# Weight conversions in twos with low parts on VectorE, gates in three steps, fillers out of S and Y, and a new planned order

## The chip, the cores and the metric

The kernel runs on one core of a Trainium2 chip, as one launch. The metric is the device time in microseconds (us). Three runs of the kernel before took 453.63, 475.21 and 476.38 us; their median is 475.21. The chip's engines work side by side, each through its own queue in order: TensorE (PE in the profile: matmuls; PEld is its weight load), VectorE (DVE), ScalarE (ACT), GpSimd (POOL), and SyncE (SP), whose queue issues the DMA transfers.

## The reference

Three computations follow each other. All inputs are float64 or float32 arrays that are computed to better than one float32 product; hence the high and low parts below.

```
# 1. mLSTM, batch 2, 8 heads, 768 steps, head width 40
m_new = max(f + m, i);  f' = exp(f + m - m_new);  i' = exp(i - m_new)
C = f' * C + i' * v k^T;   n = f' * n + i' * k
y = sigmoid(o) * (C q) / max(|n . q|, 1)
# 2. x = y as [1536, 320];  w1, w2: [320, 1024], w3: [1024, 1024], w_out: [1024, 320]
x = ((x @ w1) * (x @ w2)) @ w3 @ w_out
# 3. w_in: [320, 2048], w_out2: [2048, 320]
h = x @ w_in;   out = (h * tanh(softplus(h))) @ w_out2
```

## The kernel before, in words

**Attention in chunks.** The recurrence is cut into 6 chunks of 128 steps for each of the 2 batches: 12 units, u = 0 to 11, each with all 8 heads. The gates (running maximum, decay, sums) are scanned by VectorE once, chunk 0 first and then the other 640 columns (`part`, L612). For each unit TensorE runs these steps, in program names:

- E (L399 to L405): four matmuls of 512 columns write the exponents of the decay matrix, `psE`. Their right side `ex_r` is written per chunk by `rb` (L636). ScalarE exponentiates (`dw`).
- S (L420): eight products of keys and queries, `psS`; VectorE multiplies with the decay (`wg`).
- I (L435): what the state gives, `psI`. U (L448): the state's update, `psU`, from `vw`, which GpSimd computes; VectorE adds it to the state `st`.
- Y (L471): eight products with the values, `psY`, 41 columns each. VectorE adds I's part, ScalarE and VectorE make the divisor, GpSimd multiplies with gate and divisor (`xo`, L498: two multiplications, then a cast and a subtraction on 64 columns).
- X (L506): three transpositions, `psX`; ScalarE and VectorE split the result into a high part `hs` and a low part `ls`.

**Products.** Each fp32 product is computed as a sum of products of fp32r high and low parts. A and B (L763, L771) are x times w1 and x times w2, 8 matmuls of 512 columns each (`mm320`, L749), for 3 blocks of 4 units and 8 column groups: 24 of either. W (L722) multiplies w3 by w_out beforehand (`psw`). X1 (L785) multiplies the product of A and B with that (`psx`). H (L844, `psh`) and O (L860, `pso`) are the third computation, 48 of each, with the Mish function on ScalarE between them and one subtraction on VectorE (`gl`).

**Conversions.** Weights come as float64 words. A piece of up to 384 columns (`add_piece`, L272) is loaded by DMA (`raw`, 4 buffers), its magnitude taken (`mag`, ScalarE or VectorE) into a buffer `f` (5 buffers), clamped, put together bit by bit in three more VectorE steps (`bits1`, `bits2`, `bits3`, L296 to L309), rounded to its high part by ScalarE (`high`, L311), and subtracted by GpSimd to give the low part (`low`, L315), which frees `f`. There are 80 pieces: 16 of w1 and w2, 8 of w_out, 24 of w3, 16 of w_in2, 16 of w_out2.

**Order.** A planner (`Work`, L41) holds a node per step, with an engine, a due time (from the table `TUNE`), an assumed duration, the nodes it needs and the buffers it takes. It goes through assumed time and always picks the node that can start first, among near ones the one with the earliest due time; the order so found is emitted to each engine's queue. Where it foresees a gap on TensorE before the last X, it emits fillers (`keep_warm`, L370: matmuls of 512 columns into `psz` that nobody reads, L139 to L144). In units 0 to 5, two fillers stand inside each S and two inside each Y (L423, L474). Three more fillers stand at the start (`w0n`), after the constants that they read are made by GpSimd and ScalarE.

```
            for p in range(HP):
                if p % 2 and warm:
                    keep_warm(1)
```

## Time and profile before

| | |
|---|---|
| runs | 453.63, 475.21, 476.38 us (median 475.21) |
| profiled execution | span 474.30 us from the first to the last instruction, 0.91 less than the median; its own time is not listed |
| busy: PE, PEld | 457.97, 395.01 us |
| busy: DVE, ACT, POOL | 316.97, 196.18, 129.24 us |
| granted clock of TensorE, mean | 0.910 |

Times in the rows are from the span's start. A row of a timeline has the start, the length, the engine, the line of the kernel, the operation with the tile written and those read, the shape and the count of instructions in it; in square brackets stands idle time of the engine ahead of it, and what ended it. Matmuls overlap, so the time from one row's start to the next row's start tells what a step costs, rather than its length. A row of a window has its bounds and length, then for each engine the busy time and, in brackets, the number of instructions; then the mean granted clock of TensorE (1.00 is 2.4 GHz, 0.50 is 1.2 GHz), the share of the DMA engines and GB/s. A row of a group has the count, the busy time and the mean of one instruction in ns, and the idle time of the engine ahead of them.

### The profile page before, as it was taken

How to read it: one execution, taken by the hardware profiler on the slowest of the kernel's cores; microseconds unless marked ns; L12 is line 12 of the kernel's file. 1: busy time of each engine (PE TensorE's matmuls, PEld its weight loads, DVE VectorE, ACT ScalarE, POOL GpSimd, SP SyncE). 2: the span in 40 equal slices, each digit the busy share in tenths (PEclk: the TensorE clock that was granted, in tenths of full speed). 3: DMA queues.
4: the chain of work that ended last, by engine and by line, in shares of the span. 5: the costliest groups of instructions: out<-in, count | busy, mean ns of one | idle time of the engine just before them, and what ended most of it. 6: DMA issues, size and time to landing. Idle time of an engine off the chain costs nothing.

```text
span 474.3 us, 6843 instructions
## 1 busy us (share of the span) xinstructions
PE 458.0 (97%) x2498; PEld 395.0 (83%) x2498; DVE 317.0 (67%) x631; ACT 196.2 (41%) x404; POOL 129.2 (27%) x153
## 2 busy tenths in 40 slices
PE   7999899999889899999999999989999999999997
PEld 4687678888778789898888887869999999999996
DVE  5955856559997956887898999988994121131121
ACT  7465246533326363224443423854243322322320
POOL 3305634425645422232231252263230000000000
PEclk9659755569959999999999999999999999999999
DMA  7934435433340433233231343332301000010001
GB/s 221 273 96 122 124 117 152 123 94 119 112 117 29 141 115 100 90 102 109 78 107 62 100 134 101 101 112 75 107 29 56 2 0 1 0 57 0 1 0 55
DMA packets 31825, 41.90 MB, mean 88 GB/s; under 512 B 2160, under 2 KB 25968, under 8 KB 31792
## 3 DMA queue, kind: packets, MB, share of 16 engines
q1 hardware_dynamic: 31792, 41.48, 28.8%
q8 instruction: 19, 0.31, 0.3%
q14 instruction: 14, 0.11, 0.1%
HBM read 39.50 MB, written 1.97 MB: 87 GB/s over the span
## 4 chain that ended last, share of the span: by engine, by line
PE 45%; issue 4%; POOL 2%; DVE 1%; ACT 0%; POOLq 0%; ACTq 0%
PE pso L869 18%; PE psh L754 15%; POOL wil L212 2%; PE psa L754 2%; PE psb L754 2%; PE psx L794 2%; PE psx L796 2%; PE psx L795 2%; PE psw L729 1%; PE psx L798 1%; PE psx L799 1%; DVE pl L212 0%; DVE f L298 0%; DVE f L294 0%; DVE f L308 0%
## 5 line engine op out<-in xcount | busy, mean ns | idle before, releaser
L212 DVE TENSOR_TENSOR gl<-u,gh 128x512 fp32r<-128x512 f32 x48 | 33.9, 705 | 78.9 <-ACT u L854 76.3
L850 ACT ACTIVATE gh<-psh 128x512 fp32r<-128x512 f32 x48 | 28.6, 599 | 89.0 <-PE psh L754 85.2
L754 PE MATMUL psh<-hs,wih 128*128 128x512 f32 x144 | 56.1, 390 | 0.0
L303 DVE SCALAR_TENSOR_TENSOR f<-raw,f 128x384 int32<-128x384 int32 (+2 forms) x80 | 49.8, 623 | 1.6
L754 PE MATMUL psh<-hs,wil 128*128 128x512 f32 x144 | 48.4, 390 | 1.9 <-POOL wil L212 1.9
L308 DVE SCALAR_TENSOR_TENSOR f<-raw,f 128x384 int32<-128x384 int32 (+2 forms) x80 | 47.2, 591 | 1.3
L294 DVE TENSOR_SCALAR f<-f 128x384 f32<-128x384 f32 (+2 forms) x80 | 39.6, 500 | 7.7 <-ACT f L288 7.2
L869 PE MATMUL pso<-wo,gh 128*128 128x320 f32 x192 | 42.6, 310 | 0.0
L476 PEld LDWEIGHTS psY<-kv,w 128*128 128x128 f32 x192 | 36.9, 273 | 2.2 <-issue 0.2
L212 POOL TENSOR_TENSOR th<-f,th 128x384 fp32r<-128x384 f32 (+1 forms) x24 | 22.6, 940 | 57.8 <-ACT th L313 42.4
L298 DVE TENSOR_SCALAR f<-f 128x384 int32<-128x384 int32 (+2 forms) x80 | 36.7, 461 | 1.3
L754 PE MATMUL psh<-ls,wih 128*128 128x512 f32 x96 | 37.4, 389 | 0.0
L476 PE MATMUL psY<-kv,w 128*128 128x41 f32 x192 | 35.5, 350 | 0.0
L869 PEld LDWEIGHTS pso<-wo,gh 128*128 128x128 f32 x192 | 32.8, 188 | 1.4
L754 PEld LDWEIGHTS psh<-hs,wil 128*128 128x128 f32 x144 | 27.0, 188 | 7.9 <-POOL wil L212 2.3
L212 POOL TENSOR_TENSOR wil<-f,wih 128x384 fp32r<-128x384 f32 x16 | 23.5, 1473 | 34.5 <-ACT wih L313 31.8
L754 PE MATMUL psa<-hs,w12h 128*128 128x512 f32 x72 | 30.3, 421 | 2.0 <-DVE w L212 2.0
L729 PE MATMUL psw<-woh,th 128*128 128x320 f32 x128 | 29.2, 312 | 1.8 <-POOL th L212 0.8
L754 PEld LDWEIGHTS psh<-hs,wih 128*128 128x128 f32 x144 | 27.0, 188 | 4.3
L754 PE MATMUL psb<-hs,w12h 128*128 128x512 f32 x72 | 29.2, 405 | 1.4 <-ACT w L409 1.4
L869 PE MATMUL pso<-wo2h,gh 128*128 128x320 f32 x96 | 29.8, 310 | 0.0
L869 PE MATMUL pso<-wo2l,gh 128*128 128x320 f32 x96 | 29.7, 309 | 0.0
(131 smaller groups left out, 1054.7 us busy)
## 6 DMA issues: line engine op xcount, KB each, us to landing
raw<-in_w_dram SPq DMA_DIRECT2D x32, 384.0 KB
raw<-in_w_out_dram SPq DMA_DIRECT2D x24, 320.0 KB
raw<-in_w_in_dram SPq DMA_DIRECT2D x16, 384.0 KB
kv<-in_kv_dram SPq DMA_DIRECT2D x12, 324.0 KB
qk<-in_qk_dram SPq DMA_DIRECT2D x24, 160.0 KB
raw<-in_w_dram SPq DMA_DIRECT2D x8, 256.0 KB
sg<-in_o_gate_dram SPq DMA_DIRECT2D x12, 160.0 KB
out_dram<-yo SPq DMA_DIRECT2D x12, 160.0 KB
```

The source lines that it names most:

```text
L212: return eng.tensor_tensor(out=o, in0=a, in1=b, op=op)
L294: nc.vector.tensor_scalar(out=ff, in0=ff, scalar1=HI_MIN, scalar2=HI_MAX, op0=ALU.max, op1=ALU.min)
L298: nc.vector.tensor_scalar(out=f, in0=f, scalar1=3, scalar2=0x3FFFFFFF, op0=ALU.logical_shift_left, op1=ALU.bitwise_and)
L303: nc.vector.scalar_tensor_tensor(out=f, in0=t["raw"][:, :, 1], scalar=-0x40000000, in1=f, op0=ALU.bitwise_and, op1=ALU.bitwise_or)
L308: nc.vector.scalar_tensor_tensor(out=f, in0=t["raw"][:, :, 0], scalar=29, in1=f, op0=ALU.logical_shift_right, op1=ALU.bitwise_or)
L476: nc.tensor.matmul(ps[:, h * VW:(h + 1) * VW], lhsT=t["w"][:, h, :], rhs=t["v"][:, h, :], start=True, stop=True)
L729: nc.tensor.matmul(ps, lhsT=t[a][:, c * 128:(c + 1) * 128], rhs=wo[b], start=(c0 + c + s == 0), stop=(c0 + c == KC - 1 and s == 2))
L754: nc.tensor.matmul(ps, lhsT=a, rhs=b, start=(n == 0), stop=(n == len(seq) - 1))
L794: nc.tensor.matmul(x1ps[e], lhsT=wh, rhs=ph, start=first, stop=False)
L795: nc.tensor.matmul(x1ps[e], lhsT=wh, rhs=pl, start=False, stop=False)
L850: nc.scalar.activation(out=t["gh"], in_=t["ps"], func=AF.Mish)
L869: nc.tensor.matmul(ps, lhsT=t[a][:, sl], rhs=wo[b], start=(ft == 0 and n == 0), stop=(ft == KF2 - 1 and n == 2))
```

## The change

- Conversions go in twos: a piece is 768 columns (w1 with w2 of one column group, two groups of w_in2), 640 (two row groups of w_out or w_out2) or 512 (w3, in two parts per row group where there were three). 44 pieces instead of 80. There are 3 `raw` and 2 `f` buffers, each twice as wide; low and high parts of a piece lie in one tile.
- A table `ENG` names the engine of a step by kind of weight: low parts on VectorE but for those of w3, magnitudes on ScalarE but for w_out and the second half of w_out2.
- Gates come in three steps (chunk 0, chunk 1, chunks 2 to 5), with the subtraction that GpSimd did now on VectorE; `rb` is written in halves; the gates' i part of chunk 0 is loaded from ScalarE's queue.
- The cast and the subtraction of `xo` on GpSimd go; ScalarE copies the 64 columns (`dup`), X transposes them, and VectorE makes their low part behind X. The first multiplication (`xs`) no longer waits for the divisor.
- S and Y hold no fillers. Ten fillers at the start read a tile of zeros that VectorE writes; fillers in foreseen gaps fill 0.872 of the gap.
- The planner's assumed durations, its model of the clock and a common port for VectorE and GpSimd are changed, and all of `TUNE`: the order is new everywhere.

```diff
--- before.py
+++ after.py
...
-NRAW = 4
-NF = 5
+NRAW = 3
+NF = 2
...
-NW12A = 8
-NTH = 5
+NTH = 4
 
 TUNE = dict(
-    s_pe=0.286, s_act=0.0, s_dve=0.0, s_pool=0.0, warm=6, ahead=2, w0n=3, a0=134.03, ap=1.26,
...
+    s_pe=0.177, s_act=0.105, s_dve=0.071, s_pool=0.0, ahead=1, w0n=10, ff=0.872, ph=2.305, a0=134.03, ap=1.252,
+    a_ld=-435.054, e_e=599.147, e_s=206.636, e_r=43.484, rb=2, g_ld=-203.34, g1=-91.783, g2=-94.21, o_1=-391.129,
...
+
+ENG = dict(
+    mag_w12='ACT', mag_wo='DVE', mag_w3='ACT', mag_wi='ACT', mag_o2='ACT', mag_o3='DVE', lo_w12='DVE', lo_wo='DVE',
+    lo_w3='POOL', lo_wi='DVE', lo_o2='DVE', lo_o3='DVE', xo='POOL', vw='POOL', dup='ACT',
 )
...
+                    if self.port[n]:
+                        s = max(s, port)
...
-                while t + 2 * fill[1] < s:
-                    t, k = self.products(t, fill[1], 1.0), k + 1
+                stop = t + (s - t) * TUNE["ff"]
+                while t + 2 * fill[1] < stop:
+                    t, k = self.products(t, fill[1], 0.94), k + 1
...
-    def add_piece(due, lead, width, loads, outs, takes=(), gates=(), abs_act=True):
+    def add_piece(due, lead, width, loads, outs, takes=(), gates=(), kind=""):
...
+        mag_e, lo_e = ENG["mag_" + kind], ENG["lo_" + kind]
 
         def load():
-            t["raw"] = slot(cv, "raw", [128, 384, 2], I32)[:, 0:width]
+            t["raw"] = slot(cv, "raw", [128, 768, 2], I32)[:, 0:width]
             for o, i in loads(t["raw"]):
...
-            t["f"] = slot(cv, "f", [128, 384], I32)[:, 0:width]
-            if abs_act:
+            t["f"] = slot(cv, "f", [128, 768], I32)[:, 0:width]
+            if mag_e == "ACT":
                 nc.scalar.activation(out=t["f"].bitcast(F32), in_=t["raw"][:, :, 1].bitcast(F32), func=AF.Abs)
             else:
                 nc.vector.tensor_single_scalar(out=t["f"], in_=t["raw"][:, :, 1], scalar=0x7FFFFFFF, op=ALU.bitwise_and)
...
         def high():
-            t["h"], t["l"] = outs[0](), outs[1]()
-            nc.scalar.copy(t["h"], t["f"].bitcast(F32))
+            t["h"], t["l"] = outs()
+            nc.scalar.copy(t["h"], t["f"].bitcast(F32).rearrange("a (k c) -> a k c", k=t["h"].shape[1]))
 
         def low():
-            tt(nc.gpsimd, t["l"], t["f"].bitcast(F32), t["h"].bitcast(F32), sub)
...
-        add_node(("mag", n), "ACT" if abs_act else "DVE", due - 4, (0.41 if abs_act else 0.35) * e, mag,
-                 [("load", n), ("mag", n - 1)], [(places("f", NF), [("lo", n)])])
...
-        add_node(("lo", n), "POOL", due - 1, 0.96 * e, low, [("hi", n)])
+            eng = nc.gpsimd if lo_e == "POOL" else nc.vector
+            tt(eng, t["l"], t["f"].bitcast(F32).rearrange("a (k c) -> a k c", k=t["h"].shape[1]), t["h"].bitcast(F32), sub)
...
+        add_node(("lo", n), lo_e, due - 1, pool(width) if lo_e == "POOL" else dve(width), low, [("hi", n)], port=True)
         return n
...
-    def outs_of(pool, tag, name, width):
-        return [lambda p=p: pool().tile([128, width], F32R, tag=f"{tag}{p}", name=f"{name}{p}", bufs=1) for p in "hl"]
-
-    def cols(n, p):
-        return pieces[n][p].rearrange("a (c f) -> a c f", c=3)
+    def pair_outs(pool, tag, name, width):
+        def outs():
+            return [pool().tile([128, 2, width], F32R, tag=f"{tag}{p}", name=f"{name}{p}", bufs=1) for p in "hl"]
+        return outs
+
...
+
+        a, b = (identr, causal) if a is None else (a, b)
         ps = psum.tile([128, 512], F32, tag="b0", name="psz", bufs=1)
         for _ in range(n):
-            nc.tensor.matmul(ps, lhsT=identr, rhs=causal, start=True, stop=True)
+            nc.tensor.matmul(ps, lhsT=a, rhs=b, start=True, stop=True)
 
...
 
         def S_():
             t["S"] = [bank("psS") for _ in range(2)]
             for p in range(HP):
-                if p % 2 and warm:
-                    keep_warm(1)
                 for g in range(2):
                     rows = slice(64 * g, 64 * g + D)
...
         def Y():
             ps = t["Y"] = bank("psY")
             for h in range(H):
-                if h % 4 == 2 and warm:
-                    keep_warm(1)
                 nc.tensor.matmul(ps[:, h * VW:(h + 1) * VW], lhsT=t["w"][:, h, :], rhs=t["v"][:, h, :],
                                  start=True, stop=True)
...
-        def xo():
+        def xs():
             x = t["x"] = slot(att, "x", [128, 3 * T])
             xh = x[:, 0:DM].rearrange("a (h d) -> a h d", h=H)
-            tt(nc.gpsimd, xh, t["y"][:, :, 0:D], sg[kb, b][:, j % 2], mult)
-            tt(nc.gpsimd, xh, xh, t["r"].unsqueeze(2).to_broadcast([128, H, D]), mult)
-            nc.gpsimd.tensor_copy(out=x[:, DM:3 * T].bitcast(F32R), in_=x[:, R0:DM])
-            tt(nc.gpsimd, x[:, R0:DM], x[:, R0:DM], x[:, DM:3 * T], sub)
+            tt(nc.gpsimd if ENG["xo"] == "POOL" else nc.vector, xh, t["y"][:, :, 0:D], sg[kb, b][:, j % 2], mult)
+
+        def xo():
+            xh = t["x"][:, 0:DM].rearrange("a (h d) -> a h d", h=H)
+            tt(nc.gpsimd if ENG["xo"] == "POOL" else nc.vector, xh, xh, t["r"].unsqueeze(2).to_broadcast([128, H, D]), mult)
+
+        def dup():
+            x = t["x"]
+            if ENG["dup"] == "ACT":
+                nc.scalar.copy(x[:, DM:3 * T], x[:, R0:DM])
+            else:
+                (nc.vector if ENG["dup"] == "DVE" else nc.gpsimd).tensor_copy(out=x[:, DM:3 * T], in_=x[:, R0:DM])
...
+            half = slice(0, 64)
+            tt(nc.vector, h[half, 2, sl], p3[half, 2], h[half, 2, sl].bitcast(F32), sub)
...
+
+    STAGES = [(0, 1), (1, 2), (2, NCH)]
...
         def ld_g(c0, c1):
-            for dst, src in ((f, f_gate), (i, i_gate)):
-                nc.sync.dma_start(out=dst[:, c0 * T:c1 * T], in_=src[:, c0 * T:c1 * T])
+            for eng, dst, src in ((nc.sync, f, f_gate), (nc.sync if c0 else nc.scalar, i, i_gate)):
+                eng.dma_start(out=dst[:, c0 * T:c1 * T], in_=src[:, c0 * T:c1 * T])
 
         ld_g(0, 1)
+        nc.vector.memset(zr.bitcast(F32), 0.0)
...
+        nc.gpsimd.memset(qk[0][:, 0], 0.0)
...
-        nc.scalar.copy(identr, ident)
+        keep_warm(K["w0n"], zr[:, 0:128], zr)
...
         nc.scalar.copy(causal, z)
-        keep_warm(K["w0n"])
...
-        def rb(c):
+        def rb(c, e):
             sl = slice(c * T, (c + 1) * T)
+            hs = slice(4 * e, 4 * e + 4)
             if c >= K["rb"]:
...
-            tt(nc.vector, ex_r[c % 2][64:128], L2[64:128, sl].bitcast(F32).unsqueeze(1).to_broadcast([64, H, T]),
-               sel_h[64:128].unsqueeze(2).to_broadcast([64, H, T]), mult)
+            tt(nc.vector, ex_r[c % 2][64:128, hs], L2[64:128, sl].bitcast(F32).unsqueeze(1).to_broadcast([64, 4, T]),
+               sel_h[64:128, hs].unsqueeze(2).to_broadcast([64, 4, T]), mult)
...
+                add_node(("part", n), "DVE", due, 3 * dve(w) + dve(2 * w) + dve2(w) + (c[1] - c[0]) * dve(T), lambda c=c: part(*c),
+                         [("ld_g",), ("lb", n - 1)], port=True)
...
-    CH3 = [(0, 3), (3, 3), (6, 2)]
+    CH3 = [(0, 4), (4, 4)]
...
-        for i in range(KF2):
-            ft, x = divmod(i, 2)
-            wi_n[i] = add_piece(dues[i] - K["c_wi"], K["c_ld"], 384, cols_loads(w_in2, i),
-                                outs_of(w12_pool(ft), f"w{ft}_{x}", "wi", 384), gates=[("AB"[x], 2 * KF1 + ft)], abs_act=False)
...
+        for i in range(KF1):
+            n = add_piece(dues[2 * i] - K["c_wi"], K["c_ld"], 768, cols_loads([(w_in2, 2 * i), (w_in2, 2 * i + 1)]),
+                          pair_outs(w12_pool(i), f"w{i}", "wi", 384), gates=[(x, 2 * KF1 + i) for x in "AB"], kind="wi")
+            wi_n[2 * i], wi_n[2 * i + 1] = (n, 0), (n, 1)
...
```

How the order moves is seen at three places. The first is TensorE's queue at S of unit 0 and what follows (`psS`, `psU`, `psY` are the outputs of S, U and Y; `psz` those of fillers; `psg` transposes gates). Before:

```order
L427 MATMUL psS<-qk_78 128x128 x2
L374 MATMUL psz<-causal,identr 128x512
L427 MATMUL psS<-qk_78 128x128 x4
L374 MATMUL psz<-causal,identr 128x512
L427 MATMUL psS<-qk_78 128x128 x2
```

After:

```order
L463 MATMUL psS<-qk_78 128x128 x8
L414 MATMUL psz<-causal,identr 128x512 x4
L488 MATMUL psU<-vw,kv 40x41 x8
L414 MATMUL psz<-causal,identr 128x512 x2
L510 MATMUL psY<-kv,w 128x41 x8
L463 MATMUL psS<-qk_79 128x128 x8
L414 MATMUL psz<-causal,identr 128x512 x8
L730 MATMUL psg<-ident,gates 128x16 x4
```

The fillers moved from inside S and Y to the places between steps where the planner foresees a gap.

The second is VectorE's queue ahead of E of unit 2 (`gates` are the scanned gates, `ex_r` and `ex_l` the sides of E, L625 and L687 scan one chunk, `w` is the decay matrix). Before:

```order
L615 SCALAR_TENSOR_TENSOR gates<-gates 128x640
L212 TENSOR_TENSOR gates<-gates 128x640 x2
L620 TENSOR_SCALAR gates<-gates 128x640
L625 SCALAR_TENSOR_TENSOR gates<-gates 128x128 x5
L212 TENSOR_TENSOR w<-psS,w 128x4x128 x2
L212 TENSOR_TENSOR gates<-gates 64x640
L212 TENSOR_TENSOR gates<-gates 32x640
L212 TENSOR_TENSOR w<-psS,w 128x4x128 x2
L212 TENSOR_TENSOR ex_r_89<-gates,sel_h 64x1024
```

After:

```order
L241 TENSOR_TENSOR w<-psS,w 128x4x128 x2
L241 TENSOR_TENSOR gates<-gates 32x128
L722 SCALAR_TENSOR_TENSOR ex_l_87<-gates,sel_b,ex_l_87 32x128
L722 SCALAR_TENSOR_TENSOR ex_l_88<-gates,sel_b,ex_l_88 32x128
L241 TENSOR_TENSOR ex_r_90<-gates,sel_h 64x512
L678 SCALAR_TENSOR_TENSOR gates<-gates 128x512
L241 TENSOR_TENSOR gates<-gates 128x512 x2
L682 TENSOR_SCALAR gates<-gates 128x512
L687 SCALAR_TENSOR_TENSOR gates<-gates 128x128 x4
L241 TENSOR_TENSOR gates<-gates 128x512
L241 TENSOR_TENSOR ex_r_90<-gates,sel_h 64x512
```

Chunk 1 has its own small step ahead of the rest, but the second half of its `ex_r` still stands behind the 512-column step of the rest.

The third is the end of GpSimd's queue (`th` is the low part of a w3 piece, `wo2l` of the first half of w_out2, `wil` of w_in2, `wo_...` of the second half of w_out2). Before:

```order
L212 TENSOR_TENSOR th<-f,th 128x384 x2
L212 TENSOR_TENSOR th<-f,th 128x256
L212 TENSOR_TENSOR wo2l<-f,wo2h 128x320 x8
L212 TENSOR_TENSOR wil<-f,wih 128x384 x16
L212 TENSOR_TENSOR wo_3374<-f,wo_3374 128x320
```

After:

```order
L241 TENSOR_TENSOR x<-y,sg 128x320
L241 TENSOR_TENSOR x<-x,r 128x320
L241 TENSOR_TENSOR x<-y,sg 128x320
L241 TENSOR_TENSOR x<-x,r 128x320
L241 TENSOR_TENSOR th<-f,th 128x512 x16
```

Behind the last low part of w3 GpSimd has nothing left; what stood there is on VectorE.

## Rows read from the trace of the kernel before

**Rows 1.** Stages: length, busy us of PE, PEld, DVE, ACT, POOL; clock, DMA, GB/s.

```profile
0.00:99.88 99.88, 94.14 (x544) 75.82 (x545) 65.30 (x139) 54.48 (x118) 37.87 (x59) 0.66 0.51 150
99.88:146.15 46.27, 42.80 (x285) 37.00 (x283) 40.34 (x87) 14.22 (x36) 21.44 (x31) 0.81 0.37 112
146.15:350.00 203.85, 200.10 (x989) 171.25 (x987) 178.38 (x351) 92.16 (x186) 66.90 (x61) 1.00 0.32 97
350.00:470.95 120.95, 120.93 (x688) 110.94 (x687) 32.44 (x54) 35.32 (x67) 3.03 (x3) 1.00 0.03 12
```

**Rows 2.** Timeline of PE at the lower clock: start, us, engine, line, operation.

```profile
89.20 0.90 PE L509 MATMUL psX<-ident,x 128*128 128x128 f32 x3
89.89 1.84 PE L438 MATMUL psI<-st,qk 128*128 128x82 f32 x8
...
91.74 0.78 PE L452 MATMUL psU<-vw,kv 128*40 128x41 f32 x16
92.45 3.64 PE L476 MATMUL psY<-kv,w 128*128 128x41 f32 x16
95.89 0.77 PE L403 MATMUL psE<-causal,identr 128*128 128x512 f32 x1
...
97.87 2.08 PE L427 MATMUL psS<-qk 40*128 40x128 f32 x16
99.88 0.79 PE L754 MATMUL psa<-hs,w12h 128*128 128x512 f32 x1
```

**Rows 3.** Timeline of PE at the higher clock.

```profile
111.45 1.02 PE L438 MATMUL psI<-st,qk 128*128 128x82 f32 x8
...
112.44 0.51 PE L452 MATMUL psU<-vw,kv 128*40 128x41 f32 x16
112.88 0.50 PE L754 MATMUL psa<-hs,w12h 128*128 128x512 f32 x1
...
114.85 1.87 PE L476 MATMUL psY<-kv,w 128*128 128x41 f32 x16
116.55 0.48 PE L403 MATMUL psE<-causal,identr 128*128 128x512 f32 x1
...
117.65 1.16 PE L427 MATMUL psS<-qk 40*128 40x128 f32 x16
118.75 0.55 PE L509 MATMUL psX<-ident,x 128*128 128x128 f32 x3
```

**Rows 4.** Timeline of PE at its gap; the window 52:53 (PE, PEclk, DMA).

```profile
50.33 0.51 PE L452 MATMUL psU<-vw,kv 128*40 128x41 f32 x16 [1.37 <-DVE st L212]
...
52.00:53.00 1.00, 1.00 (x6) 0.61 0.00 0
```

**Rows 5.** The fillers alone (tile psz): PE, PEld, clock, DMA.

```profile
0.00:99.88 99.88, 26.48 (x48) 12.69 (x48) 0.66 0.51 150
```

**Rows 6.** Chain that ended last: one product A.

```profile
237.17 1.81 PE psa L754 x8
```

**Rows 7.** Timelines of DVE (gates) and PE (E of unit 2).

```profile
10.31 1.55 DVE L615 TENSOR_TENSOR_SCAN gates<-gates 128x640 f32<-128x640 f32 x1 [0.45 <-DMA gates<-in_i_gate_dram]
...
21.87 1.22 DVE L212 TENSOR_TENSOR ex_r<-gates,sel_h 64x1024 fp32r<-64x1024 f32 x1
...
32.17 0.63 PE L403 MATMUL psE<-causal,identr 128*128 128x512 f32 x1
```

**Rows 8.** Timeline of DVE: a step without and beside GpSimd; a subtraction.

```profile
298.24 0.35 DVE L298 TENSOR_SCALAR f<-f 128x384 int32<-128x384 int32 x1
...
300.48 1.15 DVE L298 TENSOR_SCALAR f<-f 128x384 int32<-128x384 int32 x1
...
302.14 0.68 DVE L212 TENSOR_TENSOR gl<-u,gh 128x512 fp32r<-128x512 f32 x1
```

**Rows 9.** Groups on GpSimd, 146.15 to 350: busy us, mean ns, idle before.

```profile
L212 POOL TENSOR_TENSOR wil<-f,wih 128x384 fp32r<-128x384 f32 x16 | 23.5, 1473 | 34.5 <-ACT wih L313 31.8 <-PE pso L869 1.6 <-PE psa L754 1.0
L212 POOL TENSOR_TENSOR th<-f,th 128x384 fp32r<-128x384 f32 x16 | 16.7, 1042 | 44.0 <-ACT th L313 31.5 <-PE psa L754 6.1 <-PE psb L754 3.5
```

More of the change, by code (lines that the diff above doesn't have):

```diff
@@ L144, in run @@
                     s = max(s, t)
+            if e == "PE" and self.form[n] != form:
+                last += self.SWITCH
+                form = self.form[n]
             free[e] = self.products(s, last, self.share[n]) if e == "PE" else s + last
             end[n] = free[e] + self.AFTER[e]
+            if self.port[n]:
+                port = free[e]
             if size:
-                dma = max(dma, s + 1.6) + max(0.45, size / 360e3)
-                end[n] = dma + 1.0
+                dma = max(dma, s + 1.6) + max(0.45, size / 287e3)
+                end[n] = dma + 0.4
             for (_, frees), p in zip(takes, got):
@@ L170, in take, with act, dve, dve2 @@
         return next(self.now)
+def act(n):
+    return 0.075 + n / 1200
+def dve(n):
+    return 0.07 + n / 960
+def dve2(n):
+    return 0.065 + n / 1920
+def pool(n):
+    return 0.03 + n * 0.00244
 SLACK = dict(PE="s_pe", ACT="s_act", DVE="s_dve", POOL="s_pool")
@@ L341, in rows_loads, with cols, rows @@
+    def cols(nk, p):
+        return pieces[nk[0]][p][:, nk[1]].rearrange("a (c f) -> a c f", c=3)
+    def rows(nk, p):
+        return pieces[nk[0]][p][:, nk[1]]
     def rows_loads(w, i):
-        return lambda raw: [(raw, words(w[i * 128:(i + 1) * 128, :]))]
+        return lambda raw: [(raw.rearrange("a (k c) w -> a k c w", k=2),
+                             words(w[i * 256:(i + 1) * 256, :]).rearrange("(k p) c w -> p k c w", k=2))]
     NU = B * NCH
@@ L558, in add_sigmoid @@
         add_node(("ld_o", i), "SP", due - 8, 0.1, load, [("ld_o", i - 1)],
-                 [(places("sg", NSG), [("xo", (2 * kb + r) * B + b) for r in range(2)])], bytes=328e3)
+                 [(places("sg", NSG), [("xs", (2 * kb + r) * B + b) for r in range(2)])], bytes=328e3)
     def add_sigmoids(which, due):
@@ L700, with w34_pair @@
     wo_n, w3_n, w12_n, wi_n, wo2_n = {}, {}, {}, {}, {}
-    def w34_tile(r, name):
-        return late["w34"].tile([128, 2 * DM], F32R, tag=f"w34_{r}", name=name, bufs=1)
+    def w34_pair(j, name):
+        return late["w34"].tile([128, 2, 2 * DM], F32R, tag=f"w34_{j}", name=name, bufs=1)
     def w3_loads(r, c0, n):
@@ L713, in add_w3, with outs @@
         c0, n = CH3[ci]
-        def out():
-            return z_slot("th")[:, 0:n * 128].bitcast(F32R)
+        def outs():
+            return [z_slot("th")[:, 0:n * 128].bitcast(F32R).rearrange("a (k c) -> a k c", k=1) for _ in range(2)]
         th = (places("z", 2 * NTH, 20), [("W", i)])
-        w3_n[i] = add_piece(due_c, K["c_ld"], n * 128, w3_loads(r, c0, n), [out, out], [th, th], [("late",)])
+        w3_n[i] = add_piece(due_c, K["c_ld"], n * 128, w3_loads(r, c0, n), outs, [th, th], [("late",)], kind="w3")
         t = pieces[w3_n[i]]
@@ L726, in W @@
             for c in range(n):
-                wo = pieces[wo_n[c0 + c]]
+                wo = {p: rows(wo_n[c0 + c], p) for p in "hl"}
                 for s, (a, b) in enumerate((("h", "h"), ("l", "h"), ("h", "l"))):
-                    nc.tensor.matmul(ps, lhsT=t[a][:, c * 128:(c + 1) * 128], rhs=wo[b], start=(c0 + c + s == 0),
+                    nc.tensor.matmul(ps, lhsT=t[a][:, 0, c * 128:(c + 1) * 128], rhs=wo[b], start=(c0 + c + s == 0),
                                      stop=(c0 + c == KC - 1 and s == 2))
         def Wh():
-            w = w34[r] = w34_tile(r, "w34")
-            nc.scalar.copy(w[:, 0:DM], tr[r][:, 0:DM])
+            if r % 2 == 0:
+                pair = w34_pair(r // 2, "w34")
+                w34[r], w34[r + 1] = pair[:, 0], pair[:, 1]
+            nc.scalar.copy(w34[r][:, 0:DM], tr[r][:, 0:DM])
         def Wl():
@@ L860, in O @@
         def O():
-            wo = pieces[wo2_n[ft]]
+            wo = {p: rows(wo2_n[ft], p) for p in "hl"}
             if ft == 0:
@@ L916 @@
             add_first(2, ft, K["p2"] + K["pp2"] * ft, K["x2"] + K["xp"] * ft)
-        for i in range(KF1):
-            wo2_n[i] = add_piece(K["c_o2"] + K["cp_o2"] * i, K["c_ld"], DM, rows_loads(w_out2, i),
-                                 outs_of(lambda: late["wo"], f"wo{i}", "wo2", DM), gates=[("W", KC * NC3 - 1)], abs_act=False)
+        for i in range(KF1 // 2):
+            n = add_piece(K["c_o2"] + K["cp_o2"] * i, K["c_ld"], 2 * DM, rows_loads(w_out2, i),
+                          pair_outs(lambda: late["wo"], f"wo{i}", "wo2", DM), gates=[("W", KC * NC3 - 1)], kind="o2")
+            wo2_n[2 * i], wo2_n[2 * i + 1] = (n, 0), (n, 1)
         dues = []
@@ L949 @@
         start()
[L950 removed]
+        work.run(dict(DVE=5.2, PE=1.3, POOL=4.7, ACT=4.8, SP=1.2, DMA=2.9), (keep_warm, 0.227, ("X", NU - 1), K["w0n"]))
         late_x.close()
```

261 lines of the change are left out of this document (143 added, 118 removed).

## The prediction

> **What bounds the kernel now.** I read the stages first [rows 1], cut where TensorE's work changes: the attention up to the first product with weights at 99.88 us, attention mixed with products up to the last transposition at 146.15, then products alone. TensorE is busy 94.14 of 99.88, 42.80 of 46.27, 200.10 of 203.85 and 120.93 of 120.95 us. So it is the bound everywhere; the reader should see in the same rows that its granted clock is not. It is 0.66 in the first stage, 0.81 in the second and 1.00 after that. There are two levels, 1.2 and 2.4 GHz, so a mean of 0.66 means 2 x 0.34 x 99.88 = 67.9 us at the lower one, and 0.81 means 17.6 us.
>
> What this costs is read from the same six steps of one head group (a unit) at either level, from the start of one step to the start of the next. At the lower level: X 0.69, I 1.85, U 0.71, Y 3.44, E 1.98, S 2.01, together 10.7 us [rows 2]. At the higher: I 0.99, U 0.44, Y 1.70, E 1.10, S 1.10 [rows 3] and X at half of 0.69, together 5.7 us. The first stage holds some 45 us of work at the higher level that takes twice as long for two thirds of it.
>
> Why the clock falls is seen at one place: U waited 1.37 us for VectorE, steps with short moving operands followed, and the granted clock went to 0.61 in the microsecond from 52 to 53, which is the fall to the lower level [rows 4]. TensorE was fully busy from then on, and the level did not return until products of 512 columns ran one behind another from 99.88. So one gap of 1.4 us cost the stretch 52 to 103 half its speed. The three runs of this kernel are 453.63, 475.21 and 476.38 us; the profiled span of 474.30 belongs to the upper two. A difference of 22 us is what that one stretch of 51 us costs if it runs at the higher level (half of 51), so I read the lower run as one in which that fall did not happen. I sum against the span of 474.30 and add the 0.91 us that separate it from the median.
>
> **The first stage.** The change takes 24 fillers out of S and Y and places 25 elsewhere between the steps; 15 at the start remain, ten of them now from a zero tile, which needs no constants from GpSimd and ScalarE. All 48 fillers were 26.48 us busy [rows 5]. Back to back they overlap; a product of eight matmuls of the same size takes 1.81 [rows 6], so a filler costs 0.23 at the higher level and 0.45 at the lower: eight fewer are worth 2 to 4 us, and where the rest stand matters more than their number.
>
> Gates in three steps: before, the scan of all 640 remaining columns started at 10.31, and the factor that E of unit 2 needs was written at 21.87; that E ran at 32.17, as TensorE at the lower level was still in Y and S of units 0 and 1 [rows 7]. Now chunk 1 comes as 128 columns ahead of the rest. VectorE's rows ahead of that E are the same work, less 1 us for the smaller step: E of unit 2 can start at about 21 us (19 if the operands land early, 24 if the two larger gate transfers, which now stand ahead of the first q/k tile on the queue, delay S of unit 0).
>
> From there to the first product TensorE has E for 8 units, U for 7, I, Y and S for 6, X for 4 and 11 fillers. By rows 3 this is 8.8 + 3.1 + 5.9 + 10.2 + 6.6 + 1.4 + 2.5 = 38.5 us, so the first product starts at 59.5; by rows 2, with fillers at 0.45, it is 15.8 + 5.0 + 11.1 + 20.6 + 12.1 + 2.8 + 5.0 = 72.4, at 93. VectorE sets its own floor: 129 of its instructions stand ahead of that place, 139 were done before in 65.30 us [rows 1], and though three double pieces replace nine single ones the sum is about the same, so nothing earlier than 65. With VectorE that full, TensorE will wait for it now and then for some tenths of a microsecond, which is just the situation of rows 4. I take the level to hold from E of unit 2 to about 48 us and to fall then: 27 of 44 us of work and waits are done, the other 14 to 17 take twice their time. The first product starts at **76** (65 to 93), against 99.88.
>
> **The second stage.** 13 products stand between the first product and the last X, where 7 did. At 1.81 each [rows 6], 10.9 us move here from the third stage. Before, 46.27 less 3.47 idle less half of 17.6 is 34.0; with the six it is 44.9. VectorE was busy 40.34 of 46.27 us, so I leave 6 for its waits and a short stay at the lower level: **51** (46 to 54). Two GpSimd steps per unit go (the cast and the subtraction on 64 columns), one ScalarE copy and one VectorE subtraction come; they lie beside TensorE's work, and if that cover is gone they cost half a microsecond per unit, 4 us in all, inside the range.
>
> **The third stage.** 324.80 us before, 3.77 of them idle; less 10.9 that moved it is 313.9. The question is whether the conversions keep up, as their low parts go to VectorE. Before, VectorE was busy 178.38 of the first 203.85 us [rows 1]. It gets 20 subtractions of 640 or 768 columns; by the 0.68 of 512 columns [rows 8], scaled, 0.8 to 1.0 each, some 18 us. It loses 24 steps of 0.35 (the magnitudes that go to ScalarE) and gets a few back, less 7. And it loses waits on GpSimd: the same step of 384 columns took 0.35 with GpSimd idle and 1.15 beside a low part there [rows 8]. GpSimd was busy 66.90 us in this stretch; what stays is 16 low parts of 512 columns at 1042 x 512/384 = 1.39 us [rows 9], 22 us, while the 16 at 1473 ns and the w_out ones go. At between a third and two thirds of a microsecond of VectorE per microsecond of GpSimd that is 15 to 30 us less. VectorE comes to 159 to 174 us in a stretch that gives it 193: it fits, with little to spare. Conversions in twos take the fixed part of an instruction half as often but bring the first low part later; TensorE waits a little more often: 2 us more, **316** (312 to 330, the upper end if each of the 8 double pieces of w_in2 comes 2 us late).
>
> The end is unchanged: 3.35 us from the last matmul at 470.95 to 474.30.
>
> Sum: 76 + 51 + 316 + 3.35 + 0.91 = **447 us**.
>
> **Rivals.**
>
> *The clock holds all the way to the first product.* Then 65 + 48 + 314 + 4.3 = 431 us. For it: fillers stand in the long gaps that the new order foresees, and the stretch of rows 3 was at the higher level with no filler in it. Against it: rows 4. The Trainium skill speaks for this rival (TensorE: Matmul & The Clock Gate, Part 1: The HAM clock gate): as it tells it, the clock falls when the engine has idled and sustained activity brings it back. By that rule a fully busy TensorE keeps its speed and 431 would be the result; the trace does not agree, as TensorE was fully busy from 52 to 100 us at the lower level. Chance 0.25.
>
> *The clock falls as early as before and returns only with the first products.* Then 93 + 53 + 318 + 4.3 = 468 us. For it: S and Y have lost the fillers that stood inside them, and S, I, U, Y and X without them are the kind of work behind which it fell at 52. Against it: fillers behind E of unit 5 make some 4 us of unbroken 512-column work, which is what brought the level back at 35 and 103. Chance 0.23 for 457 to 484.
>
> *Too few buffers: slower.* The converted-word buffers go from five of 384 columns to two of 768, raw ones from four to three. A piece holds its buffer from the magnitude on ScalarE to the end of its low part. If two pieces are in flight and the chain of one takes c, some 35 pieces remain behind the last X and need 35 c / 2. The bare steps of a 512- or 768-column piece add to some 5 to 6 us (four VectorE steps, two ScalarE steps and a low part, each 0.35 to 0.68 at 384 or 512 columns [rows 8], up to doubled), which gives 96 us, well inside 180 us of products. It decides from about 10 us per piece on, that is if every step waits a microsecond in its engine's queue behind others: at 12 us the stage takes 35 us more and the kernel 482 and up, at 13 us 500. Against it: all idle time of TensorE there was 3.77 of 324.80 us before, with GpSimd's low parts slower than VectorE's. Chance 0.10 for over 485 us.
>
> **How the numbers follow.** The forecast's own case, one fall of the clock in the middle of the first stage, has 0.42 and reaches from 438 to 457. Leaving out the lowest part of the first rival and what lies beyond the second gives 430 to 469 as the range for 8 in 10. Two per cent of 475.2 is 9.5 us, about what a measurement of this kernel can tell from no change. Faster than 465.7: 0.42 + 0.25 + 0.06 of the second rival = 0.73. Between 465.7 and 484.7: 0.17. Slower: 0.10. As the clock differs between executions of the same kernel, the runs of the changed one may well lie in two groups, some 15 us apart.
>
> **What would show it.** The first product before 80 us and a granted clock over 0.75 ahead of it; E of unit 2 at 19 to 24 us; VectorE's 384- and 512-column steps nearer to their short time; GpSimd idle after the last low part of w3; TensorE's idle time in the third stage below 8 us. Wrong would be: idle time on TensorE ahead of H with the releaser a VectorE low part (the third rival), the first product behind 90 us (the second), or no stretch at the lower level between 25 us and the first product (the first).

## The result, and the profile after

The changed kernel takes 427.08, 427.82, 427.90 and 430.40 us: a median of **427.86 us**. The ratio to the kernel before is 0.942 (95% interval 0.936 to 0.948). It is taken against the lower runs of before (453.6 and 453.9), since that kernel's runs lie in groups between 453 and 477 us; against its median of 474.67 us (24 runs, taken beside the last experiments) it is 0.901.

The stages of the profiled execution (427.82 us, span 426.0), cut at the first product, the last X and the last matmul as in [rows 1]; the columns are those of rows 1, with the third stage in two pieces:

```profile
0.00:66.34 66.34, 61.29 (x519) 51.16 (x520) 58.15 (x127) 49.72 (x111) 21.28 (x34) 0.95 0.70 214
66.34:113.40 47.06, 47.06 (x347) 41.32 (x348) 44.42 (x93) 20.00 (x44) 13.63 (x14) 1.00 0.36 118
113.40:300.00 186.60, 186.38 (x945) 162.21 (x944) 157.41 (x251) 92.72 (x153) 21.97 (x16) 1.00 0.34 108
300.00:422.01 122.01, 122.01 (x682) 110.96 (x680) 28.37 (x45) 36.96 (x68) 0.00 (x0) 1.00 0.03 11
```

| us | before | forecast | after |
|---|---|---|---|
| to the first product | 99.88 | 76 | 66.34 |
| to the last X | 46.27 | 51 | 47.06 |
| products alone | 324.80 | 316 | 308.61 |
| last matmul to the end | 3.35 | 3.35 | 3.99 |
| outside the span | 0.91 (to the median) | 0.91 | 1.82 |

The reader should see the clock column first: 0.95, 1.00, 1.00, 1.00 where before had 0.66, 0.81, 1.00, 1.00. Read microsecond by microsecond, before spends 85 us at the lower level and the changed kernel 6.8. The 48.3 us between the two spans then add up. TensorE's busy time falls from 457.97 to 416.74, by 41.2: half of 78.5 us of lower level is 39.3, and eight fillers less are about 2. Its time not busy falls from 16.3 to 9.3 us. This is a sum; no run takes away the clock's part alone.

The one stretch at the lower level begins at 27.5 us. Timeline of TensorE around it, and the clock there (length, busy time, granted clock, DMA share, GB/s):

```profile
23.20 0.50 PE L441 MATMUL psE<-causal,identr 128*128 128x512 f32 x1 [0.85 <-DVE st L503]
...
26.47 3.25 PE L510 MATMUL psY<-kv,w 128*128 128x41 f32 x16 [0.58 <-ACT ex_r L704]
29.65 2.08 PE L463 MATMUL psS<-qk 40*128 40x128 f32 x16
31.66 0.79 PE L441 MATMUL psE<-causal,identr 128*128 128x512 f32 x1
...
33.53 1.41 PE L474 MATMUL psI<-st,qk 128*128 128x82 f32 x8
34.74 0.25 PE L477 MATMUL psI<-ex_r,ones 128*128 128x8 f32 x1
34.92 0.51 PE L488 MATMUL psU<-vw,kv 128*40 128x41 f32 x16
```

```profile
26.00:28.00 2.00, 1.41 (x9) 0.88 0.12 46
28.00:30.00 2.00, 2.00 (x11) 0.50 0.01 3
30.00:34.00 4.00, 4.00 (x23) 0.50 0.26 73
34.00:38.00 4.00, 4.00 (x48) 0.96 0.68 205
```

Two waits of 0.85 and 0.58 us stand ahead of the fall, as the wait of 1.37 us did before [rows 4]. The difference is what follows: before, the level stayed down for 51 us; here it is back at 34.3 us, inside the I that runs right behind E.

### The profile page after: what moved, and what is told of

It reads as the page before. It is cut to its first block, busy times and chain, and to the rows that moved or that the text cites. A ratio compares the mean times of both kernels' runs of the same rounds, so it can differ in the third digit from the quotient of the medians.

```text
span 426.0 us, 6481 instructions
## 1 busy us (share of the span) xinstructions
PE 416.7 (98%) x2489; PEld 365.6 (86%) x2489; DVE 288.9 (68%) x516; ACT 199.4 (47%) x374; POOL 56.9 (13%) x64
## 4 chain that ended last, share of the span: by engine, by line
PE 81%; DVE 12%; ACT 2%; DMA 1%; issue 1%; SPq 0%; DVEq 0%
PE psh L834 20%; PE pso L949 20%; PE psa L834 9%; PE psb L834 9%; PE psw L807 7%; PE psY L510 4%; PE psS L463 3%; PE psI L474 2%; DMA gates<-in_i_gate_dram 1%; PE psx L875 1%; PE psx L876 1%; PE psx L874 1%; DVE pl L241 1%; DVE f L333 1%; PE psE L441 1%
## 5 line engine op out<-in xcount | busy, mean ns | idle before, releaser
L834 PE MATMUL psh<-hs,wil 128*128 128x512 f32 x144 | 48.3, 389 | 0.0
L333 DVE SCALAR_TENSOR_TENSOR f<-raw,f 128x768 int32<-128x768 int32 (+2 forms) x44 | 39.7, 904 | 0.4
L318 ACT ACTIVATE f<-raw 128x768 f32<-128x768 f32 (+2 forms) x36 | 28.5, 796 | 24.0 <-POOL th L241 10.4
L338 DVE SCALAR_TENSOR_TENSOR f<-raw,f 128x768 int32<-128x768 int32 (+2 forms) x44 | 39.4, 898 | 0.2
L834 PE MATMUL psh<-ls,wih 128*128 128x512 f32 x96 | 37.4, 389 | 0.0
L949 PE MATMUL pso<-wo,gl 128*128 128x320 f32 x96 | 29.8, 310 | 0.0
L949 PE MATMUL pso<-wo2h,gh 128*128 128x320 f32 x96 | 29.8, 310 | 0.0
L949 PE MATMUL pso<-wo2h,gl 128*128 128x320 f32 x96 | 29.7, 309 | 0.0
L241 POOL TENSOR_TENSOR th<-f,th 128x512 fp32r<-128x512 f32 x16 | 22.0, 1373 | 57.7 <-ACT th L343 53.7
L834 PE MATMUL psa<-hs,w12h 128*128 128x512 f32 x72 | 28.5, 397 | 0.8 <-DVE st L241 0.8
L934 ACT ACTIVATE u<-psh 128x512 f32<-128x512 f32 x48 | 28.5, 594 | 0.0
L834 PE MATMUL psb<-hs,w12h 128*128 128x512 f32 x72 | 28.5, 395 | 0.0
L807 PE MATMUL psw<-woh,th 128*128 128x320 f32 x128 | 28.3, 309 | 0.0
L328 DVE TENSOR_SCALAR f<-f 128x768 int32<-128x768 int32 (+2 forms) x44 | 26.9, 613 | 0.4
```

The costliest lines, as they stand in the source:

```text
L241: return eng.tensor_tensor(out=o, in0=a, in1=b, op=op)
L318: nc.scalar.activation(out=t["f"].bitcast(F32), in_=t["raw"][:, :, 1].bitcast(F32), func=AF.Abs)
L328: nc.vector.tensor_scalar(out=f, in0=f, scalar1=3, scalar2=0x3FFFFFFF, op0=ALU.logical_shift_left, op1=ALU.bitwise_and)
L333: nc.vector.scalar_tensor_tensor(out=f, in0=t["raw"][:, :, 1], scalar=-0x40000000, in1=f, op0=ALU.bitwise_and, op1=ALU.bitwise_or)
L338: nc.vector.scalar_tensor_tensor(out=f, in0=t["raw"][:, :, 0], scalar=29, in1=f, op0=ALU.logical_shift_right, op1=ALU.bitwise_or)
L807: nc.tensor.matmul(ps, lhsT=t[a][:, 0, c * 128:(c + 1) * 128], rhs=wo[b], start=(c0 + c + s == 0), stop=(c0 + c == KC - 1 and s == 2))
```

## The experiments

**Which fillers matter?** Three kernels change the fillers of the changed kernel and leave every other order as it is.

```diff
             for p in range(HP):                       # fill_in_SY, and the same inside Y
+                if p % 2 and u < 6:
+                    keep_warm(1)
...
-                fill[0](n)                            # no_gap_fill
+                pass
...
-        keep_warm(K["w0n"], zr[:, 0:128], zr)         # no_zero_fill
```

> The changed kernel with the 24 fillers back inside S and Y of units 0 to 5; order of everything else unchanged. Theory 1 (taking them out was worth their own time and the clock does not need them): 24 x 0.23 = 5.5 us less what falls into waits of TensorE, so 430 to 433 us against 427.9, and the one stretch at the lower level (27.8 to 34.6 us) stays. Rival (they hold the clock): that stretch goes, 3.4 us come back, and the time is 427 to 430.

434.46 us (433.01 to 434.81), a little over the end of theory 1's range. Stage 1 grows by 7.0 us to 73.3; E of unit 2 comes at 26.15 instead of 20.00. The stretch at the lower level does not go, it moves to 12.6 to 19.4 us and is as long as before (6.8 us). So these fillers cost their own time and did not hold the level. The rival falls.

> The changed kernel without the 30 fillers in foreseen gaps; the ten at the start stay; order unchanged. Theory 1 (these fillers hold the clock): the granted clock falls between 10 and 20 us and is at the lower level for 20 to 50 us of the attention; 437 to 452 us. Rival (the shorter waits of the new order hold it, fillers or not): no more than the one short stretch, 425 to 430.

429.67 us (429.51 to 430.63), and both are partly wrong. The clock does fall more, as theory 1 says, 20.5 us in two stretches, but the price is 1.8 us. Stages 1 and 2 of this kernel:

```profile
0.00:68.28 68.28, 59.20 (x490) 49.99 (x490) 58.44 (x127) 49.92 (x111) 22.17 (x34) 0.85 0.67 209
68.28:115.30 47.02, 47.02 (x347) 41.30 (x348) 44.41 (x93) 19.96 (x44) 13.61 (x14) 1.00 0.35 117
```

The first stretch, from 13 to 23, costs nothing: E of unit 2 runs at 19.56, earlier than with fillers. In the chain of the changed kernel that ended last, the pieces from 19.7 to 26.9 us are VectorE's (gates, `ex_r`, `ex_l`, `w`): up to there TensorE's level is hidden. The second stretch, 40.4 to 50.7, costs 5.1 us, and S and Y wait 1.14 and 1.34 us where fillers stood; 10 fillers saved behind 27 us (2.3 us) and the missing stretch of 27.5 to 34.3 (3.4 us) pay most of it back. Both stretches end after 10.2 us, with no filler in them.

> The changed kernel without the ten fillers from the zero tile at the start. Theory 1 (early work keeps the level that the program starts with): TensorE idles to 6 us, the level falls before 15 us and some 10 to 20 us run at half speed; 432 to 438 us. Rival (the start does not matter, as before held the level to 14.7 us with its first work at 3.2): 426 to 429.

427.46 us (426.87 to 427.85): the rival. TensorE starts at 4.28 instead of 1.45, S of unit 0 at 10.14 instead of 10.47. The only stretch that the column shows at the lower level, from 29.8 us, lasts 3.4 us.

**What are the low parts on VectorE worth?** All of them on GpSimd, first in the order as planned, then planned anew for it:

```diff
-            eng = nc.gpsimd if lo_e == "POOL" else nc.vector      # low_on_pool
+            eng = nc.gpsimd
...
-    mag_w12='ACT', mag_wo='DVE', mag_w3='ACT', mag_wi='ACT', mag_o2='ACT', mag_o3='DVE', lo_w12='DVE', lo_wo='DVE',
-    lo_w3='POOL', lo_wi='DVE', lo_o2='DVE', lo_o3='DVE', xo='POOL', vw='POOL', dup='ACT',    # low_on_pool_planned
+    mag_w12='ACT', mag_wo='DVE', mag_w3='ACT', mag_wi='ACT', mag_o2='ACT', mag_o3='DVE', lo_w12='POOL', lo_wo='POOL',
+    lo_w3='POOL', lo_wi='POOL', lo_o2='POOL', lo_o3='POOL', xo='POOL', vw='POOL', dup='ACT',
```

> The changed kernel with all low parts on GpSimd, in the planned order. Theory 1 (the low parts on VectorE are worth something because a GpSimd low part is long, holds one of two buffers and slows VectorE's steps beside it): each of 28 pieces gets 1.5 to 2 us longer, TensorE waits for pieces behind the last X and before the first product; 440 to 460 us. Rival (hidden behind TensorE's products anyway, as TensorE idled only 0.2 us in that stage): 426 to 430.

> The changed kernel with all low parts on GpSimd, planned anew for it. Theory 1 (two buffers and a long low part set the pace of the conversions wherever they stand in the order; it took 441.6 with the order unchanged): 436 to 445 us. Rival (only the order was unsuited): 427 to 432.

441.58 us (439.12 to 445.44) and 440.64 us (440.38 to 440.77): theory 1 by its times, in either order; the waits are only in part those that it names. Stages of the first, and TensorE's longest waits (total us, times, longest):

```profile
0.00:66.50 66.50, 62.07 (x520) 52.01 (x520) 56.74 (x124) 49.97 (x111) 25.35 (x37) 0.92 0.69 212
66.50:114.80 48.30, 47.13 (x347) 41.36 (x348) 44.81 (x88) 19.56 (x44) 22.19 (x19) 1.00 0.37 117
114.80:300.00 185.20, 177.77 (x875) 152.08 (x875) 156.42 (x228) 89.15 (x147) 60.69 (x36) 0.99 0.34 108
```

```profile
PE psx L875 <- DVE pl L241: 3.2, 3, 2.2
PE pso L949 <- DVE gl L241: 2.1, 1, 2.1
...
PE psx L874 <- ACT ph L860: 1.4, 1, 1.4
```

The first product does not move; 10.8 of the 12.2 us of span are lost behind the last X. TensorE is idle 7.4 of 185.2 us there where it was idle 0.2, and another fall of the clock, from 277.1 to 280.5 us, costs 1.7. VectorE lost 23 instructions in that stretch and is busy almost as long (156.42 against 157.41 us), so its other steps got longer while GpSimd was busy 60.69 us instead of 21.97. The largest growth is in the low parts of the products of A and B (`pl`). In the third stage of the changed kernel and of low_on_pool:

```profile
L241 DVE TENSOR_TENSOR pl<-a,ph 128x512 fp32r<-128x512 f32 x24 | 16.4, 685 | 0.1
```

```profile
L241 DVE TENSOR_TENSOR pl<-a,ph 128x512 fp32r<-128x512 f32 x24 | 24.1, 1008 | 1.8 <-ACT ph L860 1.7
```

TensorE's waits are for `pl`, `gl` and `ph`; only one, of 0.8 us, is for the low part of a weight piece on GpSimd (`th`). So theory 1's third reason, a slower VectorE, shows in the waits, and pieces that come late hardly do.

**Gates in two steps**, planned anew:

```diff
-    STAGES = [(0, 1), (1, 2), (2, NCH)]
+    STAGES = [(0, 1), (1, NCH)]
...
```

> The changed kernel with the gates in two steps as before (chunk 0, then chunks 1 to 5), planned anew. Theory 1 (E of unit 2 comes later, TensorE fills the time, VectorE's chain behind it moves by as much): first product 2 to 4 us later, 429 to 433 us against 427.9. Rival (VectorE's total sets the first stage, not when chunk 1 is ready): 427 to 429.

435.3 us (435.25 to 441.32), worse than theory 1, and not where it says: the first product is at 65.2, but TensorE waits 4.3 us for `hs` of an X and 1.4 us for `ls`, the level falls three times between 45 and 73 us, and the last X ends at 121.6 instead of 113.4. As the planner moved other steps too, this doesn't say what the third step alone is worth; that stays open.

**One part of the change alone, on the kernel before:** no fillers inside S and Y.

```diff
-                if p % 2 and warm:
+                if p % 2 and warm and False:          # and the same in Y
```

> The kernel before without the 24 fillers inside S and Y of units 0 to 5; order unchanged: one part of the change alone. Theory 1 (the level held for another reason, the order; these fillers neither hold nor restore it): 24 fillers less, at 0.23 to 0.45 us each, some at the lower level, 6 to 10 us: 464 to 469 us where the kernel before takes 475. Rival (they hold it up in the stretch from 35 to 52 us): the level is lost from 35 us on, 8 us are paid for the 6 to 10 saved: 472 to 480.

464.71 us (462.13 to 465.29): theory 1. Its level is at 0.67 in stage 1, like before's 0.66, and the first product comes at 88.1 instead of 99.9. Its long stretch at the lower level, 43.9 to 91.7 us, lasts 47.8 us, so the fillers inside S and Y are not what keeps that kernel's level down.

**What brought the level of the kernel before down, and what kept it there?** Three small edits of that kernel, each at one place:

```diff
+            if u == 4:                                # before_wait_filled: ahead of U of unit 4
+                keep_warm(6)
             ps = t["U"] = bank("psU")
...
+            if u == 6:                                # before_fill_once: behind E of unit 6
+                keep_warm(8)
...
+        for a, b in zip(pe, pe[1:]):                  # before_S_ahead_of_E: neighbours on TensorE
+            if not isinstance(a, int) and not isinstance(b, int) and a[0] == "E" and b[0] == "S" and a[1] >= 6:
+                i, j = seq.index(a), seq.index(b)
...
+                seq.insert(j, seq.pop(i))
...
```

> The kernel before with six fillers ahead of U of unit 4, in its wait of 1.37 us for VectorE at 49 us. Theory 1 (that wait brings the level down, for want of work just there): no fall at 52, first product at 75 to 80 us, 452 to 457 us in every run. Rival (the short-operand steps behind it bring it down anyway): the level falls some microseconds later, 466 to 476.

453.76 us (451.79 to 456.01, 10 runs) where the kernel before takes 474.67 (453.25 to 476.90, 24 runs beside them). Theory 1. The place of [rows 4] in this kernel:

```profile
48.54 0.49 PE L511 MATMUL psX<-ident,x 128*128 128x128 f32 x3
48.79 1.64 PE L374 MATMUL psz<-causal,identr 128*128 128x512 f32 x6
50.47 0.51 PE L454 MATMUL psU<-vw,kv 128*40 128x41 f32 x16
```

```profile
50.00:52.00 2.00, 1.94 (x27) 1.00 0.60 212
52.00:54.00 2.00, 2.00 (x17) 1.00 0.00 0
54.00:56.00 2.00, 2.00 (x18) 1.00 0.69 215
```

U starts as late as before; only the wait is filled. The level stays, and the first product comes at 81.2 instead of 99.88. Six fillers in a wait of 1.4 us are worth 21 us against that median.

> The kernel before with eight more fillers right behind E of unit 6 (60 us, in the middle of its long stretch at the lower level). Theory 1 (a run of 512-column matmuls brings the level back, and what that kernel lacks between 52 and 103 us is such a run; the level explains its 22 us): back within 8 us, the rest of the stretch to 103 us runs at the higher level, 456 to 462 us instead of 475. Rival (VectorE or latency sets that stretch, or the level falls again at once): 474 to 480.

462.88 us (458.83 to 464.63): theory 1, 0.9 us over its range. Start of the fillers and of the next step:

```profile
61.80 3.37 PE L374 MATMUL psz<-causal,identr 128*128 128x512 f32 x8
65.10 0.49 PE L429 MATMUL psS<-qk 40*128 40x128 f32 x4
```

The level is back at 64.7 us, during the fillers, and stays to 88.6; the fall there follows a wait of 1.9 us for VectorE.

> The kernel before with E of units 6 to 11 put behind the S that followed it, so that X and I follow E directly, as they do in the changed kernel; nothing else moved. Theory 1 (at the lower level the long operands must stand together: E with X and I behind it brings the level back, as in the changed kernel at 32 to 35 us, E with S behind it does not): back by 76 us at the latest, 456 to 464 us instead of 475. Rival (which step stands beside E does not matter): 474 to 477.

459.97 us (456.23 to 465.75, 10 runs): theory 1 by its times. Of 24 runs of before beside it 17 are above 470 us, of these 10 none is above 466. The mechanism itself is not shown: in the profiled execution the level did not fall at all at that place, though the wait ahead of U was there:

```profile
48.43 0.51 PE L459 MATMUL psU<-vw,kv 128*40 128x41 f32 x16 [1.36 <-DVE st L219]
...
57.15 0.50 PE L410 MATMUL psE<-causal,identr 128*128 128x512 f32 x1
...
58.17 0.49 PE L516 MATMUL psX<-ident,x 128*128 128x128 f32 x3
```

So the same wait is followed by a fall in one execution and not in another. That the order decides how much a fall costs fits the ten times, but no trace shows it: by their mean clocks (0.963 to 0.937) those runs spent some 34 to 58 us at the lower level, against 85 in the profiled execution of before, and how that divides into falls stays open.

**Two attempts to go further.** Fillers in the two waits ahead of 27.5 us, and the low parts of w1 and w2 alone on GpSimd:

```diff
+                if u == 3 and e == 1:                 # two_waits_filled: inside E
+                    keep_warm(4)
+            if u == 1:                                # ahead of Y
+                keep_warm(3)
...
-    mag_w12='ACT', mag_wo='DVE', mag_w3='ACT', mag_wi='ACT', mag_o2='ACT', mag_o3='DVE', lo_w12='DVE', lo_wo='DVE',
+    mag_w12='ACT', mag_wo='DVE', mag_w3='ACT', mag_wi='ACT', mag_o2='ACT', mag_o3='DVE', lo_w12='POOL', lo_wo='DVE',
...                                                   # w12_low_on_pool
```

> The changed kernel with four fillers in the wait of 0.85 us inside E of unit 3 and three in that of 0.58 us ahead of Y of unit 1. Theory 1 (these waits bring the level down at 27.8 us, but VectorE sets the first stage): the stretch at the lower level goes, the first product comes 0 to 2 us earlier, 426 to 428 us. Rival (TensorE sets the first stage): half of 6.8 us comes back, 424 to 425.

426.87 us (426.26 to 427.95, 6 runs; ratio to before 0.941, 0.939 to 0.944), not to be told from the changed kernel. The level no longer falls at 27.5 but at 34.2, behind a wait of 0.61 us ahead of the next Y, for the same 6.8 us, so the first product is at 66.4. Neither theory was tested: the fall went elsewhere.

> The changed kernel with the low parts of w1 and w2 alone on GpSimd, which is idle for two thirds of the first stage, planned anew. Theory 1 (VectorE sets the first stage; 8 subtractions of 0.9 us come off it, half of them ahead of the first product): 424 to 427 us. Rival (a low part of 2.9 us on GpSimd holds one of two buffers, and slows VectorE beside it): 428 to 433.

430.57 us (429.98 to 435.05, 6 runs): the rival by its time, not by its mechanism.

```profile
0.00:59.70 59.70, 52.97 (x482) 44.17 (x482) 52.39 (x116) 45.65 (x101) 24.41 (x36) 1.00 0.72 218
59.70:116.30 56.60, 53.50 (x383) 46.59 (x384) 47.32 (x97) 23.47 (x54) 23.65 (x21) 0.94 0.41 128
```

The first product comes 6.6 us earlier with 37 matmuls fewer ahead of it. TensorE waits 1.5 us for `hs` just ahead of it and 3.1 us for `ls` behind its first matmul, and the level falls during the second wait. What the first stage gave back the second took, and 2.9 us more. The low parts took 1.83 us each on GpSimd rather than the rival's 2.9, and none ran there between 54 and 64.9 us, where those waits are; VectorE was busy with conversion steps and the decay ahead of `ls`. The planner had moved other steps too, so what the engine alone is worth stays open.

## Why the prediction was right and wrong

**The total.** 447 us was forecast and 427.86 measured, 2 us below the end of the range (430 to 469). The direction was right; that 447 of 475.21 is the 0.941 that the ratio shows is an accident, because the ratio's base is the lower runs. The first rival, 431 us at a chance of 0.25, was the better forecast: 65 + 48 + 314 + 4.3 stands against 66.3 + 47.1 + 308.6 + 5.8.

**The step that failed** is "I take the level to hold from E of unit 2 to about 48 us and to fall then", with 14 to 17 us of work at half speed up to the first product. The level fell at 27.5 us, for as small a cause as foreseen, and came back 6.8 us later; that costs 3.4 us where 14 to 17 were put down. I had taken from [rows 1] and [rows 4] that a fall lasts until products come. In these runs only the old order, Y, E, S, X, I, U, shows that, with its fillers inside S and Y (51 us) and without them (47.8). With eight fillers at one place of it, the level came back (before_fill_once), and with S ahead of E no run was in the upper group. In the new order E mostly stands between S and X or I, and no fall in the nine traces of the changed kernel and its variants lasted longer than 10.2 us. Why a fall is short there is argued from the order and not shown: the one run that changes it alone had no fall at that place in its profiled execution. The rival's own sign, no lower stretch behind 25 us, did not come either: it is not that the clock holds, but that it returns. The reason that I gave for the rival, fillers in the gaps, is wrong: without them the time is 429.67.

By the Trainium skill (TensorE: Matmul & The Clock Gate, Part 1: The HAM clock gate) the level falls when the engine has idled. The runs stand between that and my reading of rows 4. Filling the wait keeps the level up, as that rule would have it (before_wait_filled). But falls came behind waits of only 0.6 to 1.4 us, and TensorE was fully busy again when the level fell (Y from 26.47 us, the fall at 27.5); one wait of 1.36 us did not bring it (before_S_ahead_of_E). And by that rule activity brings the level back, where the order before kept a fully busy engine at the lower one for 51 us.

**What the lower run of before meant** is borne out in the main: filling the wait ahead of the stretch behind 52 us turns every run into one like the lower (453.76). But no lower run of before has a trace. Their mean clock of 0.974 over 452 us means some 24 us at the lower level where the profiled execution had 85, so more than that one stretch of 51 us was missing in them.

**VectorE's floor of 65 us** held to the number (66.3) and not in its reason. In the chain that ended last VectorE has the path from 11.7 to 27 us, again from 37.4 to 43.3, and, behind ScalarE, from 64.6 to the first product; TensorE has 28.5 of the 39.4 us behind 27, at the higher level for all but 6.8. Pieces of that chain:

```profile
35.43 1.92 PE psY L510 x16
...
37.37 0.50 DVE y L241
...
42.09 1.21 DVE w L241 x2
...
43.34 1.75 PE psY L510 x14
...
61.47 1.06 ACT w L447 x2
...
65.86 0.34 DVE st L241
```

VectorE's own work ahead of the first product came to 58.15 us in 127 instructions where 65 was taken; the two engines in turn set the 66.3. w12_low_on_pool came below it with a smaller share of work ahead of the first product.

**E of unit 2** was forecast at 21 us (19 to 24) and ran at 20.00:

```profile
20.00 0.50 PE L441 MATMUL psE<-causal,identr 128*128 128x512 f32 x1
```

**The fillers out of S and Y.** "Where the rest stand matters more than their number" was wrong as well. Taken out they are worth 6.6 us in the new kernel and 10 in the old; the 30 in foreseen gaps together are worth 1.8.

**The second stage** was 47.06 against 51: the 13 products took what they should, 44.9 us by the working, and only 2 of the 6 us left for waits and a fall were needed. The two GpSimd steps less per unit, costed at nothing, left no wait.

**The third stage** was 308.6 against 316 (312 to 330). The 10.9 us that moved out did so; most of the rest is TensorE's idle time, 0.2 us where I had 3.77 plus 2. That conversions fit was right, and VectorE had more relief than forecast: 185.8 us in this stage against 210.8, 25 less where the terms (+18, -7, -15 to -30) gave 4 to 19. Some of it may only have moved: VectorE is busy 4.1 us more in the second stage. GpSimd has the 22 us that were costed and nothing behind the last w3 piece. By line, on GpSimd and then on VectorE behind it:

```profile
L241 POOL TENSOR_TENSOR th<-f,th 128x512 fp32r<-128x512 f32 x16 | 22.0, 1373 | 57.7 <-ACT th L343 53.7
```

```profile
L328 DVE TENSOR_SCALAR f<-f 128x512 int32<-128x512 int32 x16 | 11.0, 688 | 0.3
...
L328 DVE TENSOR_SCALAR f<-f 128x768 int32<-128x768 int32 x8 | 4.3, 554 | 0.0
```

On the mean the same step takes 688 ns on 512 columns in the time of w3's low parts and 554 ns on 768 columns when GpSimd has none. That is in line with rows 8 (0.35 and 1.15 us). What all low parts on GpSimd cost, with everything that follows from it, low_on_pool shows: 13 to 14 us.

**Too few buffers** was nearer than I thought. I had put a piece's chain at 5 to 6 us with 10 as the point from which it decides. The 16 low parts of w3 start between 129.27 and 190.50 us, 4.08 us apart; ScalarE waited 10.4 us in 12 of the magnitudes for a low part to free `f`:

```profile
ACT f L318 <- POOL th L241: 10.4, 12, 1.5
```

With two buffers that is a chain of up to 8.2 us. It cost no product here; with the other low parts on GpSimd TensorE waited once, 0.8 us, for such a low part.

**Runs in two groups**, some 15 us apart, did not come: the four lie within 3.3 us. Short falls would explain that. And the 0.91 us between span and time belonged to a median of other executions; within one execution it is 1.8 (427.82 against 426.0).

## What to carry to other kernels

Where a clock level or a state doubles the price of all work, look for the single wait that loses it, and fill that wait: six matmuls nobody reads were worth 21 us in the kernel before, while 24 of them spread over the steps cost 10. Then look at how long a fall lasts, not only how often it comes: 51 us in the old order, 10.2 at most in the new one, with the order of the steps as the likely, unproven reason. And when work moves to an engine that looks idle, look at the steps that run beside it: with 28 low parts moved to GpSimd, VectorE did fewer instructions in the third stage and was busy as long.
